# Transposing y one slot later and running the MLP's second product two pieces behind its first

## The chip, the core and the metric

The kernel runs on one core of one Trainium2 chip. The metric is device time in microseconds for one whole call, given as the median of several runs; the span from the first instruction to the last is a little shorter. The engines that matter here are TensorE (PE in the profile; its weight loads are a row of their own, PEld), VectorE (DVE), ScalarE (ACT) and GpSimd (POOL). SyncE (SP) issues most transfers.

## What is computed

Three layers follow one another on 3072 tokens of width 320 (batch 4, 768 steps, 8 heads of 40): a recurrence with a state per head, an MLP whose activation is the square of relu, and a mixture of 8 experts with one expert per token.

```python
# recurrence, per batch and head, for t in 0..767
y[t]   = r[t] @ state
Sa     = state @ a[t]
state  = state * w[t][None, :] - outer(Sa, b[t]) + outer(v[t], k[t])

# MLP, w_in 320x2048, w_out 2048x320
h = x @ w_in
g = np.maximum(h, 0.0) ** 2
x = g @ w_out

# mixture: 8 experts, capacity 768, w1 320x1024, w2 1024x320
expert = argmax(x @ w_gate); gate = softmax(x @ w_gate)[expert]
out = gate * (relu(x_e @ w1[expert]) @ w2[expert])
```

All values are float32. The products of MLP and experts are formed from high and low parts: a number is split into a rounded high part (written by ScalarE as fp32r) and the rest (subtracted on VectorE), and three of the four partial products are added.

## The kernel before

**Recurrence (class `Rwkv`).** The 768 steps are cut into 12 segments `s` of 64 steps, and a segment into two chunks `c` of 32 steps. In a chunk the steps are solved together, for which each segment needs the inverse of a triangular 32x32 matrix per head and batch. `invert` (from L194) forms it on GpSimd: 31 steps, each a product (`tmp`) and a subtraction (`solve_tl`), all recorded at L289 and all chained to one another. Ahead of it stands `lower` (from L173): PE makes `pa`, ACT copies a part of it (`solve_ab`, L185) and DVE masks and transposes it (`am`, L187; `a`, L191; `solve_al`, L198). Behind it, `inverted` (L214) transposes the result on DVE (`solve_tf`, L219) into `tt` (L222, L223), and `solve` applies it (`psa`). The state is carried on by `zv`, `zk`, `pz`, `pn` and `psd`. `products` (L116) prepares the decays of a coming segment by two scans on DVE: `rq_r` (L124, followed by a clamp L133 and a reciprocal L134) and `rq_q` (L137). `out` makes y of a chunk: `py` on PE, `y` on DVE (L388).

**MLP (class `Mlp`).** The 256 tokens of a segment (64 steps, 4 batches) go through 8 pieces `fp` of 256 hidden columns. `add_y` turns y by three transposes on PE (`pt`, L454) and splits it (ACT L459 to L461, DVE L462, L463). `up` makes a piece's first product in two halves of 8 matmuls (`pl`, L447), then relu on ACT (L645), relu times `pl` on DVE (`g`, L647), and its split: `gh` on ACT (L409), `gl` on DVE (L410). `down` makes the second product in two halves of 6 matmuls (`acc`, L629), with the high weights `woh` and a transferred low part `wol`. It runs one piece behind `up` (`self.last`). `gh` and `gl` have two buffers each, which the conversion of weights at the start also uses (`a`, `raw`, `mh`, `ml`, L517 to L551).

**Mixture (class `Moe`).** 15 units of 256 gathered tokens, with its own `up` and `down` (`upl`, `uacc`), which take over the same one-piece delay.

**What sets the order.** Only TensorE's instructions keep the program's order (`keep_in_program_order`), and GpSimd's are chained one behind another (`issue_after`). On DVE and ACT a scheduler chooses the order when the kernel is built. The main loop has slots `slot_a` to `slot_g` for each chunk; after each, `mlp(n)` puts in `n` halves of MLP pieces, by the table `SLOTS` (`SECOND` for segment 1, `FIRST` for 0). So TensorE alternates between recurrence and MLP. After the last segment the remaining pieces of the MLP run beside the routing of the tokens, then the mixture alone.

Of the kernel before, what the change touches and what calls it, by code (L numbers as in the profile page):

```python
# [30 lines left out]
C = 32  # L31
# [41 lines left out]
class Rwkv:  # L73
# [6 lines left out]
    def __init__(self, ctx, tc, ps, consts, keep, wd, kb, ad, rv, wl, tok, vt, rng):  # L80
        self.tc, self.nc, self.ps = tc, tc.nc, ps
        self.c = consts
        self.src = dict(wd=wd, kb=kb, ad=ad, rv=rv, wl=wl, tok=tok, vt=vt)
        nc = self.nc
        p1 = ctx.enter_context(tc.tile_pool(name="rw1", bufs=1))
        self.p = ctx.enter_context(tc.tile_pool(name="rwr", bufs=1))
# [127 lines left out]
    def inverted(self, s):  # L214
# [6 lines left out]
        tt = self.tile([128, C, NC, H], f"tt.{s}", 2)  # L221
# [159 lines left out]
    def out(self, s, c):  # L381
# [5 lines left out]
        y = self.tile([128, DM + 64], f"y.{s}_{c}", 2)  # L387
# [82 lines left out]
class Mlp:  # L470
# [28 lines left out]
    def tile(self, shape, name, tag, bufs, dt=F32):  # L499
        return self.p.tile(shape, dt, tag=tag, name=name, bufs=bufs)  # L500
# [101 lines left out]
    def load_gate(self):  # L602
        self.turn = self.routed = self.done = 0
        self.wo = {}
        self.last = self.slow = self.behind = None
# [30 lines left out]
    def up(self, s, x, fp, wol):  # L636
# [10 lines left out]
        nc.vector.tensor_tensor(out=g, in0=pl, in1=g, op=ALU.mult)  # L647
        gh = self.tile([128, 2, NT], f"gh{s}_{fp}", "gh", 2, F32R)
        gl = self.tile([128, 2, NT], f"gl{s}_{fp}", "gl", 2, F32R)
        self.behind = split(nc, gh, gl, g)  # L650
        self.last = partial(self.down, s, fp, gh, gl, wol)
        yield

    def down(self, s, fp, gh, gl, wol):
        if fp == 0:
            self.acc = [self.psa.tile([128, DX], F32, tag=f"acc{t}", name=f"acc{s}_{t}") for t in range(2)]
        for f in range(2):
            ft = fp * 2 + f
            for t in range(2):
                cols = slice(t * 128, (t + 1) * 128)  # L660
                for n, (a, b) in enumerate(((gh, self.woh[:, ft]), (gl, self.woh[:, ft]), (gh, wol[:, f]))):
                    self.mm(self.acc[t], lhsT=a[:, f, cols], rhs=b,
                            start=ft == 0 and n == 0, stop=ft == NFT - 1 and n == 2)
# [17 lines left out]
    def bursts(self, s, x):  # L681


        for fp in range(NFT // 2):
            last = self.last
            yield from self.routers(2 * fp + 2)
            yield from self.up(s, x, fp, self.low(s, fp))
            if last:
                yield from last()


class Slow:
# [53 lines left out]
    def mlp(self, ctx, y, w_in, w_out, w_gate, x1, logits):  # L746
# [13 lines left out]
        with tc.tile_pool(name="slm", bufs=2) as p, tc.For_i(0, NS, 1) as s:  # L760
# [10 lines left out]
            for fp in range(NFT // 2):  # L771
                for _ in ml.up("f", x, fp, ml.low("f", fp)):
                    pass
                for _ in ml.last():
# [3 lines left out]
        ml.last = ml.behind = None  # L778
# [3 lines left out]
class Moe:  # L782
# [426 lines left out]
    def unit(self, j, units):  # L1209
# [7 lines left out]
        for fp in range(FE // 256):  # L1217
# [3 lines left out]
            last, ml.last = ml.last, partial(self.down, j, w2, h, fp)  # L1221
            yield
            if last:
                yield from last()
# [7 lines left out]
    def run(self, units):  # L1232
        if not self.ml.last:
# [8 lines left out]
        for _ in self.ml.last():  # L1242
            pass
        self.ml.last = None
# [17 lines left out]
def const_arrays():  # L1262
# [5 lines left out]
        ident=np.eye(128),  # L1268
        mlow=s[None, :] < t[:, None],
        mup=t[:, None] < s[None, :],  # L1270
        lane=np.ones((128, 1)),
# [16 lines left out]
    for n, parts in enumerate((one, two)):  # L1288
# [8 lines left out]
AHEAD = 5000  # L1297
USUAL = 15
FIRST_UNITS, NE = 3, 10
# [36 lines left out]
def tile_rwkv__mlp__moe(ctx, tc, wd, kb, ad, rv, wl, tok, vt, nat, w_in, w_out, w_gate, w1, w2, cap, cst1, cst2, out):  # L1336
# [9 lines left out]
    with ExitStack() as ph:  # L1346
# [4 lines left out]
        rw = Rwkv(rp, tc, ps, consts, keep, wd, kb, ad, rv, wl, tok, vt, rng)  # L1351
# [48 lines left out]
        for s in range(NS):  # L1400
# [3 lines left out]
            for c in range(NC):  # L1404
                last, y = ys, None
                more = s + 1 < NS

                def others(half):
# [22 lines left out]
                def slot_c():  # L1431
                    if s > 1:
# [6 lines left out]
                def slot_d():  # L1439
                    rw.turn(s, c)  # L1440
# [129 lines left out]
_INS = ["wd", "kb", "ad", "rv", "wl", "tok", "vt", "nat", "w_in", "w_out", "w_gate", "w1", "w2", "cap", "cst1", "cst2"]  # L1570
# [3 lines left out]
def arrays(inputs):  # L1574
# [6 lines left out]
    d["cst1"], d["cst2"] = const_arrays()  # L1581
# [20 lines left out]
```

## Time and profile before

| what | value |
|---|---|
| median of 3 runs | 1127.3 us (1125.11 to 1129.19) |
| the profiled execution, its own time | 1132.63 us |
| its span (first to last instruction) | 1130.8 us |
| mean granted TensorE clock | 0.937 of full speed |
| busy: PE, PEld, DVE, ACT, POOL | 914.1, 854.5, 848.6, 570.4, 537.8 us |

The page gives busy time by engine and, for groups of instructions, the idle time of the engine ahead of them with what ended it. Idle time alone is no cost: it counts only where it lies on the chain of work that ends last. The table of the chain of waits follows that chain back from the last instruction. A timeline lists instructions in order of start, with the idle time of the engine before one in brackets and what released it. "x2" means that two instructions of one kind are listed as one row.

### The profile page before, as it was taken

The page shows a single profiled execution, that of the slowest core. Times are in us where ns is not written, and L with a number is a line of the kernel's source. Part 1 is how long each engine was busy: PE and PEld are TensorE (multiplying, and loading weights), DVE is VectorE, ACT ScalarE, POOL GpSimd, SP SyncE. Part 2 cuts the span into 40 slices and gives each one's busy share as a digit, 9 for nine tenths or more (in the row PEclk, how much of TensorE's full clock was granted, in tenths as well). Part 3 has the DMA queues.
Part 4 walks back from the last instruction along what each step waited for, and adds up shares of the span by engine and source line. Part 5 has one row for each costly group of instructions (what it writes and reads, how often), then busy time and mean ns, then how long its engine had stood idle before and what let it go on. Part 6 is the DMA issues. An engine that isn't in the chain of part 4 may idle for free.

```text
span 1130.8 us, 38768 instructions
## 1 busy us (share of the span) xinstructions
PE 914.1 (81%) x15962; PEld 854.5 (76%) x15962; DVE 848.6 (75%) x1807; ACT 570.4 (50%) x1570; POOL 537.8 (48%) x866
## 2 busy tenths in 40 slices
PE   1645535877988979797989798999999998999992
PEld 1545435767877969687978788899989998899992
DVE  7868966678787877778786878757777967777860
ACT  2435424444454454454545454555464667667750
POOL 4793851818385765739393939380010132223220
PEclk9999997988898989888988899999999999999997
DMA  8833634843353534443544345344194576677720
GB/s 225 217 95 103 154 96 119 275 126 114 107 158 102 163 100 136 126 115 108 152 120 135 119 123 152 98 121 119 56 327 120 161 220 191 195 209 236 226 80 9
DMA packets 85968, 164.19 MB, mean 145 GB/s; under 512 B 15565, under 2 KB 45903, under 8 KB 84816
## 3 DMA queue, kind: packets, MB, share of 16 engines
q1 hardware_dynamic: 76848, 141.52, 43.1%
q10 hardware_dynamic: 6048, 11.06, 3.6%
q0 software_dynamic: 2880, 8.98, 2.3%
q8 instruction: 129, 2.11, 0.8%
q14 instruction: 63, 0.52, 0.2%
HBM read 137.34 MB, written 16.24 MB: 136 GB/s over the span
## 4 chain that ended last, share of the span: by engine, by line
POOL 37%; PE 26%; DVE 12%; issue 9%; DMA 7%; ACT 3%; SPq 0%; POOLq 0%; DVEq 0%; ACTq 0%
POOL solve_tl L289 19%; POOL tmp L289 18%; PE upl L447 6%; PE uacc L1127 6%; PE pl L447 5%; PE acc L629 4%; DMA out_dram<-uo,room 4%; DMA xg<-x_dram,room 2%; DVE a L191 1%; PE pa L292 1%; DVE zv L348 1%; DVE solve_tf L219 1%; DVE g L647 1%; DVE gl L410 1%; DVE a L348 1%
## 5 line engine op out<-in xcount | busy, mean ns | idle before, releaser
L289 POOL TENSOR_TENSOR solve_tl<-solve_tl,tmp 128x126 f32<-128x126 f32 (+22 forms) x372 | 229.2, 616 | 29.1
L289 POOL TENSOR_TENSOR tmp<-solve_al,solve_tl 128x126 f32<-128x126 f32 (+22 forms) x372 | 210.2, 565 | 39.9 <-DVE a L191 11.7
L629 PE MATMUL acc<-woh,gh 128*128 128x328 f32 x384 | 134.5, 350 | 52.1 <-ACT gh L409 51.5
L629 PE MATMUL acc<-woh,gl 128*128 128x328 f32 x384 | 129.9, 338 | 12.7 <-DVE gl L410 12.1
L629 PE MATMUL acc<-wol,gh 128*128 128x328 f32 x384 | 126.5, 329 | 0.0
L447 PE MATMUL pl<-x_lo,wi_hi 128*128 128x256 f32 x384 | 113.3, 295 | 14.0 <-DVE x_lo L462 14.0
L447 PE MATMUL pl<-x_hi,wi_hi 128*128 128x256 f32 x384 | 120.4, 313 | 0.7 <-ACT x_hi L459 0.7
L629 PEld LDWEIGHTS acc<-woh,gh 128*128 128x128 f32 x384 | 77.5, 202 | 57.3 <-ACT gh L409 53.9
L447 PE MATMUL pl<-x_hi,wi_lo 128*128 128x256 f32 x384 | 112.9, 294 | 0.0
L1205 POOL DMA_INDIRECT out_dram<-uo,room x30 | 33.8, 1125 | 153.3 <-DVE uo L1194 82.7
L647 DVE TENSOR_TENSOR g<-pl,g 128x512 f32<-128x512 f32 x96 | 65.7, 684 | 49.2 <-ACT g L645 48.8
L645 ACT ACTIVATE g<-pl 128x512 f32<-128x512 f32 x96 | 57.2, 596 | 86.7 <-PE pl L447 85.0
L410 DVE TENSOR_TENSOR gl<-g,gh 128x512 fp32r<-128x512 f32 x96 | 66.6, 694 | 43.9 <-ACT gh L409 43.5
L289 POOL MEMSET solve_tl<- 128x512 f32 x12 | 6.8, 563 | 194.0 <-DVE solve_al L198 177.5
L409 ACT CAST gh<-g 128x512 fp32r<-128x512 f32 x96 | 59.3, 618 | 73.4 <-DVE g L647 69.7
L1135 POOL DMA_INDIRECT xg<-x_dram,room x30 | 30.5, 1017 | 135.1 <-DVE room L967 56.1
L629 PEld LDWEIGHTS acc<-woh,gl 128*128 128x128 f32 x384 | 78.0, 203 | 19.5 <-DVE gl L410 19.2
L447 PEld LDWEIGHTS pl<-x_lo,wi_hi 128*128 128x128 f32 x384 | 77.7, 202 | 14.3 <-DVE x_lo L462 14.3
L1127 PE MATMUL uacc<-w2h,hh 128*128 128x320 f32 x240 | 76.9, 320 | 10.5 <-DVE uo L1194 9.1
L447 PEld LDWEIGHTS pl<-x_hi,wi_hi 128*128 128x128 f32 x384 | 77.3, 201 | 4.5 <-ACT x_hi L459 1.1
L629 PEld LDWEIGHTS acc<-wol,gh 128*128 128x128 f32 x384 | 78.2, 204 | 0.0
L447 PEld LDWEIGHTS pl<-x_hi,wi_lo 128*128 128x128 f32 x384 | 77.6, 202 | 0.0
(263 smaller groups left out, 2783.9 us busy)
## 6 DMA issues: line engine op xcount, KB each, us to landing
wol<-wol SPq DMA_DIRECT2D x96, 328.0 KB
w<-in_w_dram SPq DMA_DIRECT2D x30, 640.0 KB
w<-in_w_dram SPq DMA_DIRECT2D x30, 512.0 KB
zv<-in_vt_dram SPq DMA_DIRECT2D x48, 208.0 KB
kb_d<-in_kb_dram SPq DMA_DIRECT2D x24, 320.0 KB
zk<-in_tok_dram SPq DMA_DIRECT2D x48, 160.0 KB
rx<-rt SPq DMA_DIRECT2D x192, 40.0 KB
w<-in_w_dram SPq DMA_DIRECT2D x30, 256.0 KB
```

The costliest lines, as they stand in the source:

```text
L191: nc.vector.transpose(out=ak[:, 0], in_=am[BY_STEP[j]])
L289: self.last = f(*a, **k).ins
L348: self.nc.vector.tensor_mul(v, v, w)
L409: return (nc.scalar.copy(hi, x).ins, nc.vector.tensor_tensor(out=lo, in0=x, in1=hi.bitcast(F32), op=ALU.subtract).ins)
L410: nc.vector.tensor_tensor(out=lo, in0=x, in1=hi.bitcast(F32), op=ALU.subtract).ins)
L447: tc.keep_in_program_order(tc.nc.tensor.matmul(out, lhsT=a, rhs=b, start=n == 0, stop=n == len(seq) - 1))
L629: self.tc.keep_in_program_order(self.nc.tensor.matmul(*a, **k))
L645: nc.scalar.activation(g, pl, AF.Relu)
L647: nc.vector.tensor_tensor(out=g, in0=pl, in1=g, op=ALU.mult)
L1127: self.tc.keep_in_program_order(self.nc.tensor.matmul(*a, **k))
L1135: nc.gpsimd.indirect_dma_start(out=xg[:, 0:DX], out_offset=None, in_=self.x1, in_offset=bass.IndirectOffsetOnAxis(ap=self.idx[2 * j + t], ...
L1205: self.nc.gpsimd.indirect_dma_start(out=self.out, out_offset=bass.IndirectOffsetOnAxis(ap=self.to[:, n:n + 1], axis=0), in_=o[:, t], in_of ...
```

## The change

1. `add_y` of a chunk moves from `slot_b`, ahead of `solve`, to `slot_c` for chunk 0 (ahead of `lower`) and to `slot_d` for chunk 1. In segment 1, chunk 0 it stays. `y` and `tt` go from two buffers to one.
2. `down` runs two pieces behind `up` (`BEHIND = 2`, a list `pending`); in the mixture the delay stays at one piece (`drain(1)`), so that after the mixture's first `up` two pieces of `down` stand in a row. Within `down`, the order is now `gh` by high and low weights for both halves of the tokens, then `gl`. The transfer of `wol` is issued one burst later, still one piece ahead of its use.
3. ACT squares relu straight into `gh`. DVE's product for `g` comes behind that (it overwrites relu), then `gl`. ACT and DVE keep their counts of operations.
4. `gh` and `gl` get three buffers. Some constants move into an array of their own (`cst3`, 128x70), loaded on ACT's queue.

```diff
+        ct = p1.tile([128, cst.shape[1]], F32, name="ct3")
+        nc.scalar.dma_start(out=ct, in_=cst)
...
-        tt = self.tile([128, C, NC, H], f"tt.{s}", 2)
+        tt = self.tile([128, C, NC, H], f"tt.{s}", 1)
...
-        y = self.tile([128, DM + 64], f"y.{s}_{c}", 2)
+        y = self.tile([128, DM + 64], f"y.{s}_{c}", 1)
...
     def tile(self, shape, name, tag, bufs, dt=F32):
+        bufs = BUFS.get(tag, bufs)
...
-        nc.vector.tensor_tensor(out=g, in0=pl, in1=g, op=ALU.mult)
         gh = self.tile([128, 2, NT], f"gh{s}_{fp}", "gh", 2, F32R)
         gl = self.tile([128, 2, NT], f"gl{s}_{fp}", "gl", 2, F32R)
-        self.behind = split(nc, gh, gl, g)
-        self.last = partial(self.down, s, fp, gh, gl, wol)
+        square = nc.scalar.activation(gh, g, AF.Square).ins
+        nc.vector.tensor_tensor(out=g, in0=pl, in1=g, op=ALU.mult)
+        self.behind = (square, nc.vector.tensor_tensor(out=gl, in0=g, in1=gh.bitcast(F32), op=ALU.subtract).ins)
+        self.pending.append([self.down, s, fp, gh, gl, None])
...
-            for t in range(2):
-                cols = slice(t * 128, (t + 1) * 128)
-                for n, (a, b) in enumerate(((gh, self.woh[:, ft]), (gl, self.woh[:, ft]), (gh, wol[:, f]))):
...
+            parts = (0, gh, self.woh[:, ft]), (1, gh, wol[:, f]), (2, gl, self.woh[:, ft])
+            for n, a, b, t in [(*p, t) for ps in (parts[:2], parts[2:]) for t in range(2) for p in ps]:
...
-            last = self.last
             yield from self.routers(2 * fp + 2)
-            yield from self.up(s, x, fp, self.low(s, fp))
-            if last:
-                yield from last()
+            self.lows()
+            yield from self.up(s, x, fp)
+            yield from self.drain(BEHIND)
+
+    def drain(self, n):
+
+        while len(self.pending) > n:
+            self.lows()
+            f, *a = self.pending.pop(0)
+            yield from f(*a)
...
+BUFS = dict(gh=3, gl=3)
+BEHIND = 2
...
                 def slot_b():
-                    if y is not None:
-                        ml.add_y(xs[last[0]], last[1], y)
+                    nonlocal y
                     if s == 1 and c == 0:
+                        add()
+                        y = None
...
                 def slot_c():
+                    add()
                     if s > 1:
...
                 def slot_d():
+                    if c == 1:
+                        add()
                     rw.turn(s, c)
```

TensorE around the solution of segment 7, before: `acc5` is the second product of the MLP for segment 5, `pt` turns y, `psa7` applies the inverse, `pz` belongs to the state.

```order
L629 MATMUL acc5_0_7615<-wol5_5_7981,gh5_5_8075 128x328
L629 MATMUL acc5_1_7616<-woh_88,gh5_5_8075 128x328
L629 MATMUL acc5_1_7616<-woh_88,gl5_5_8076 128x328
L629 MATMUL acc5_1_7616<-wol5_5_7981,gh5_5_8075 128x328
L454 MATMUL pt_8252<-ct_60,y_6_1_8202 128x128 x3
L292 MATMUL psa7_0_8261<-rh_7_0_8238,tt_7_8125 32x40 x32
L270 MATMUL pz6_1_0_0_8301<-ct_60,zv0_114 104x40
L270 MATMUL pz6_1_0_1_8302<-ct_60,zv0_114 104x40
```

The same place after: half a piece of the first product (`pl5_7`) stands ahead of `psa7`, whose line is now L294.

```order
L449 MATMUL pl5_7_8242<-x_hi_5990,wi_lo_492 128x256
L449 MATMUL pl5_7_8242<-x_mx_5992,wi_mx_493 128x256
L449 MATMUL pl5_7_8242<-tops0_99,wi_mx_493 128x256
L294 MATMUL psa7_0_8251<-rh_7_0_8234,tt_7_8121 32x40 x32
L272 MATMUL pz6_1_0_0_8291<-ct_60,zv0_116 104x40
L272 MATMUL pz6_1_0_1_8292<-ct_60,zv0_116 104x40
```

The turning of y follows some rows later, behind 8 matmuls of `pl5_7` and 12 of `acc5`, and directly ahead of `pa8`, which starts the next inverse:

```order
L633 MATMUL acc5_1_7682<-wol5_5_8067,gh5_5_7990 128x328
L633 MATMUL acc5_0_7681<-woh_88,gl5_5_7991 128x328
L633 MATMUL acc5_1_7682<-woh_88,gl5_5_7991 128x328
L456 MATMUL pt_8334<-ct_60,y_6_1_8198 128x128 x3
L294 MATMUL pa8_0_8344<-kb_d_113,a0_114 32x64 x32
L294 MATMUL pa8_1_8385<-kb_d_113,a0_114 32x64 x32
```

Between `pz` and `pa8` there were 16 matmuls of `pl` and 6 of `acc` before; now it is 8, 12 and the three transposes.

VectorE from the end of inverse 7 on, before (order's rows call a scan SCALAR_TENSOR_TENSOR; `rq10_q8` and `rq16_r9` are the scans, and stand ahead of these rows):

```order
L219 STREAM_TRANSPOSE solve_tf7_8123<-solve_tl7_7346 128x1024
L647 TENSOR_TENSOR g5_6_8153<-pl5_6_8136,g5_6_8153 128x512
L388 TENSOR_TENSOR y_6_1_8202<-py6_1_8169,qt_6_1_7077 128x320
L223 SCALAR_TENSOR_TENSOR tt_7_8125<-solve_tf7_8123,ct_60,tt_7_8125 128x512
L243 STREAM_TRANSPOSE qt_8_0_9246<-rq10_q8_8797 128x8x32
L244 STREAM_TRANSPOSE qt_8_0_9246<-rq10_q8_8797 128x8x8
L410 TENSOR_TENSOR gl5_6_8157<-g5_6_8153,gh5_6_8156 128x512
L348 TENSOR_TENSOR zv0_114<-zv0_114,g64_7_6883 40x8x2x40 x2
L282 TENSOR_TENSOR zk1_120<-zk1_120,rx_7_1_8690 64x2x8x40 x2
```

The same engine and place after:

```order
L221 STREAM_TRANSPOSE solve_tf7_8119<-solve_tl7_7342 128x1024
L245 STREAM_TRANSPOSE rt_8_1_8793<-rq10_r8_8586 128x8x32
L246 STREAM_TRANSPOSE rt_8_1_8793<-rq10_r8_8586 128x8x8
L139 SCALAR_TENSOR_TENSOR rq10_q8_8796<-wl_8_8065,seed_q_111 128x650
L225 SCALAR_TENSOR_TENSOR tt_7_8121<-solve_tf7_8119,ct3_106,tt_7_8121 128x512
L123 MEMSET seed_q_111 104x16
L660 TENSOR_TENSOR g5_6_8141<-pl5_6_8124,g5_6_8141 128x512
L390 TENSOR_TENSOR y_6_1_8198<-py6_1_8165,qt_6_1_7073 128x320
L126 SCALAR_TENSOR_TENSOR rq16_r9_8803<-w_d_112,seed_q_111 104x1040
L661 TENSOR_TENSOR gl5_6_8144<-g5_6_8141,gh5_6_8143 128x512
L350 TENSOR_TENSOR zv0_116<-zv0_116,g64_7_6879 40x8x2x40 x2
L284 TENSOR_TENSOR zk1_122<-zk1_122,rx_7_1_8676 64x2x8x40
```

The scans, with two transposes, a memset, a clamp and a reciprocal that belong to them, have moved from ahead of `solve_tf` to behind it. It is so for the inverses 3 to 9; after inverse 10 only `rq10_q` has moved.

## Rows read from the trace of the kernel before

**Rows 1.** Page, chain that ended last: share of the span by engine.

```profile
POOL 37%; PE 26%; DVE 12%; issue 9%; DMA 7%; ACT 3%; SPq 0%; POOLq 0%; DVEq 0%; ACTq 0%
```

**Rows 2.** Waits of PE, 200 to 720 us: total us, times, longest.

```profile
PE acc L629 <- ACT gh L409: 35.9, 9, 4.8
PE pt L454 <- DVE y L388: 12.5, 7, 4.9
```

**Rows 3.** Timeline of POOL: first product of inverses 3 and 8.

```profile
252.78 0.24 POOL L289 TENSOR_TENSOR tmp<-solve_al,solve_tl 128x31 f32<-128x31 f32 x1 [1.68 <-DVE a L191]
555.45 0.24 POOL L289 TENSOR_TENSOR tmp<-solve_al,solve_tl 128x31 f32<-128x31 f32 x1 [0.35 <-DVE a L191]
```

**Rows 4.** Windows: us; busy PE, PEld, DVE, ACT, POOL; PEclk; DMA; GB/s.

```profile
555.45:597.71 42.26, 35.94 (x834) 32.81 (x833) 33.26 (x51) 18.89 (x46) 37.47 (x62) 0.92 0.52 149
676.25:715.60 39.35, 35.65 (x833) 32.76 (x832) 29.50 (x48) 18.01 (x45) 34.56 (x62) 0.96 0.50 144
477.57:496.79 19.22, 16.30 (x331) 14.71 (x330) 14.44 (x25) 11.55 (x31) 0.87 (x4) 0.82 0.38 103
538.86:555.45 16.59, 15.65 (x464) 14.64 (x454) 14.23 (x25) 11.45 (x31) 1.05 (x4) 1.00 0.40 111
527.58:533.25 5.67, 5.67 (x122) 5.38 (x114) 5.45 (x8) 1.73 (x6) 5.36 (x5) 0.71 0.50 149
830.00:834.00 4.00, 3.74 (x17) 3.47 (x17) 3.31 (x13) 3.14 (x11) 0.00 (x0) 0.65 1.05 393
```

**Rows 5.** Timeline of DVE between inverses 7 and 8.

```profile
539.08 1.25 DVE L219 STREAM_TRANSPOSE solve_tf<-solve_tl 128x1024 f32<-128x1024 f32 x1 [1.09 <-POOL solve_tl L289]
...
547.99 0.69 DVE L647 TENSOR_TENSOR g<-pl,g 128x512 f32<-128x512 f32 x1 [0.97 <-ACT g L645]
549.37 0.69 DVE L410 TENSOR_TENSOR gl<-g,gh 128x512 fp32r<-128x512 f32 x1 [0.68 <-ACT gh L409]
```

**Rows 6.** Timeline of DVE inside inverse 7: the two scans.

```profile
528.18 1.61 DVE L137 TENSOR_TENSOR_SCAN rq_q<-wl,seed_q 128x650 f32<-128x650 f32 x1
...
529.98 2.33 DVE L124 TENSOR_TENSOR_SCAN rq_r<-w_d,seed_q 104x1040 f32<-104x1040 f32 x1
```

**Rows 7.** Timeline of POOL at the same time.

```profile
527.57 0.40 POOL L289 TENSOR_TENSOR solve_tl<-solve_tl,tmp 128x110 f32<-128x110 f32 x1
...
528.50 1.50 POOL L289 TENSOR_TENSOR solve_tl<-solve_tl,tmp 128x108 f32<-128x108 f32 x1
530.08 2.37 POOL L289 TENSOR_TENSOR tmp<-solve_al,solve_tl 128x96 f32<-128x96 f32 x1
532.53 0.77 POOL L289 TENSOR_TENSOR solve_tl<-solve_tl,tmp 128x96 f32<-128x96 f32 x1
```

**Rows 8.** Timeline of DVE between inverses 1 and 2, while POOL is idle.

```profile
161.90 0.41 DVE L520 SCALAR_TENSOR_TENSOR a<-raw,a 128x256 uint32<-128x256 uint32 x1
...
165.89 1.50 DVE L137 TENSOR_TENSOR_SCAN rq_q<-wl,seed_q 128x650 f32<-128x650 f32 x1
...
169.24 2.32 DVE L124 TENSOR_TENSOR_SCAN rq_r<-w_d,seed_q 104x1040 f32<-104x1040 f32 x1
```

**Rows 9.** Timeline of PE between inverses 6 and 7.

```profile
481.44 0.73 PE L454 MATMUL pt<-ct,y 128*128 128x128 f32 x3 [2.21 <-DVE y L388]
...
484.82 0.58 PE L447 MATMUL pl<-x_hi,wi_hi 128*128 128x256 f32 x1
...
488.40 0.47 PE L629 MATMUL acc<-woh,gh 128*128 128x328 f32 x1
...
490.08 1.99 PE L292 MATMUL pa<-kb_d,a 40*32 40x64 f32 x128
```

**Rows 10.** Waits of PE, 817 to 862 us.

```profile
PE acc L629 <- ACT gh L409: 2.8, 2, 1.7
PE acc L629 <- DVE gl L410: 0.9, 3, 0.3
```

**Rows 11.** Timeline of PE between inverses 1 and 2.

```profile
181.08 0.64 PE L629 MATMUL acc<-woh,gh 128*128 128x328 f32 x1 [12.76 <-ACT gh L409]
```

More of the change, by code (lines that the diff above doesn't have):

```diff
@@ L604, in load_gate @@
         self.wo = {}
-        self.last = self.slow = self.behind = None
+        self.slow = self.behind = None
+        self.pending = []
         for k in range(3):
@@ L634, in low, with lows, up @@
         return wol
-    def up(self, s, x, fp, wol):
+    def lows(self):
+        for p in self.pending:
+            if p[-1] is None:
+                p[-1] = self.low(*p[1:3])
+    def up(self, s, x, fp):
         nc, NT = self.nc, self.NT
@@ L658, in down @@
             ft = fp * 2 + f
-            for t in range(2):
-                cols = slice(t * 128, (t + 1) * 128)
-                for n, (a, b) in enumerate(((gh, self.woh[:, ft]), (gl, self.woh[:, ft]), (gh, wol[:, f]))):
-                    self.mm(self.acc[t], lhsT=a[:, f, cols], rhs=b,
-                            start=ft == 0 and n == 0, stop=ft == NFT - 1 and n == 2)
+            parts = (0, gh, self.woh[:, ft]), (1, gh, wol[:, f]), (2, gl, self.woh[:, ft])
+            for n, a, b, t in [(*p, t) for ps in (parts[:2], parts[2:]) for t in range(2) for p in ps]:
+                self.mm(self.acc[t], lhsT=a[:, f, t * 128:(t + 1) * 128], rhs=b,
+                        start=ft == 0 and n == 0, stop=ft == NFT - 1 and n == 2)
             if f == 0:
@@ L771, in mlp @@
             for fp in range(NFT // 2):
-                for _ in ml.up("f", x, fp, ml.low("f", fp)):
+                for _ in ml.up("f", x, fp):
                     pass
-                for _ in ml.last():
+                for _ in ml.drain(0):
                     pass
@@ L777, in mlp @@
         nc.sync.dma_start(out=logits, in_=lgd)
-        ml.last = ml.behind = None
+        ml.behind = None
         return ps, ml
@@ L1220, in unit @@
             h = self.up(j, x, w, fp)
-            last, ml.last = ml.last, partial(self.down, j, w2, h, fp)
+            ml.lows()
+            ml.pending.append([self.down, j, w2, h, fp])
             yield
-            if last:
-                yield from last()
+            yield from ml.drain(1)
             for _ in range(5):
@@ L1232, in run @@
     def run(self, units):
-        if not self.ml.last:
+        if not self.ml.pending:
             self.ml.behind = None
@@ L1241, in run @@
             yield from self.unit(j, units)
-        for _ in self.ml.last():
+        for _ in self.ml.drain(0):
             pass
-        self.ml.last = None
     def others(self):
@@ L1268, in const_arrays @@
         ident=np.eye(128),
+        lane=np.ones((128, 1)),
+    )
+    own = dict(
         mlow=s[None, :] < t[:, None],
         mup=t[:, None] < s[None, :],
-        lane=np.ones((128, 1)),
         par=np.stack([p // 16 % 2 == 0, p // 16 % 2 == 1], axis=1),
@@ L1287, in const_arrays @@
     out = []
-    for n, parts in enumerate((one, two)):
+    for n, parts in enumerate((one, two, own)):
         at = 0
@@ L1350, in tile_rwkv__mlp__moe @@
         rp = ph.enter_context(ExitStack())
-        rw = Rwkv(rp, tc, ps, consts, keep, wd, kb, ad, rv, wl, tok, vt, rng)
+        rw = Rwkv(rp, tc, ps, consts, keep, wd, kb, ad, rv, wl, tok, vt, rng, cst3)
         xs = {}
@@ L1406, in tile_rwkv__mlp__moe, with add @@
                 more = s + 1 < NS
+                def add():
+                    if y is not None:
+                        ml.add_y(xs[last[0]], last[1], y)
                 def others(half):
```

10 lines of the change are left out of this document (5 added, 5 removed).

## The prediction

> **What bounds the kernel now.** I began with the chain that ended last. GpSimd holds 37% of the span and TensorE 26% [rows 1], and the GpSimd part is the 31-step inverse. So the kernel has two stages: until the last inverse ends, the loop through GpSimd sets the pace; behind it, TensorE does.
>
> The loop next. The first product of inverse 3 starts at 252.78 us, that of inverse 8 at 555.45 [rows 3]. Five segments take 302.7 us, 60.5 each. A whole inverse lasts 42.3 us (the first line of [rows 4]), so 18.2 us are left between the end of one and the start of the next. I call that stretch the gap: the result is turned, `psa` and the state follow, then `pa`, its transposes, and GpSimd starts again. One gap took 16.6 us at full TensorE clock, another 19.2 us at a mean granted clock of 0.82 [rows 4].
>
> Then TensorE's waits in these segments: 35.9 us in 9 waits for `gh`, 12.5 us for y [rows 2]. They look like the prize, but the longest wait for `gh`, 4.8 us, and its kind lie while GpSimd works on an inverse, so that its end doesn't lead to the next start. What counts is what lies in the gap, and what lengthens the inverse.
>
> **Steady segments, the gap.** In the gap between inverses 7 and 8 DVE works 14.2 of 16.6 us [rows 4]: DVE is the engine that sets it at full clock. Its two waits in the middle, 0.97 and 0.68 us, are for relu and `gh` of the piece being made [rows 5]. With half a piece ahead of `psa`, `pl` ends 8 matmuls sooner, and relu and square lie beside DVE's work on `zk`; I take both waits away: -1.65. The order of the changed kernel puts both scans, with their clamp, reciprocal, transposes and memset, into the gap. Before, that run of instructions took 5.67 us (from 527.58 on, [rows 4]). It stood beside GpSimd there; with GpSimd idle the two scans take 1.50 and 2.32 us [rows 8] against 1.61 and 2.33 [rows 6], so I take 5.5. The gap becomes 16.6 - 1.65 + 5.5 = 20.4 us at full clock. The scans' inputs are ready long before, so none waits; but `tt` waits for the first scan, and all that hangs on `tt` and `zv` (`psa`, `pz`) starts 2 and 4 us later.
>
> That idles TensorE. Its work ahead of `psa` is 6 `acc` and 8 `pl`, about 2 us, while DVE needs 1.2 (`solve_tf`), 0.6 (transposes), 1.5 (scan) and 0.7 (`tt`); between `psa` and `pz` it waits again, for the second scan. In the gap of rows 9 an idle time of 2.21 us went before, and the 16 `pl` took from 484.82 to 488.40, 0.22 us each, the 6 `acc` 0.28 us each [rows 9], with a granted clock of 0.82 over the gap: the lower of the two levels, 1.2 GHz, while they ran. If that happens after the change, `pz` ends about 10.1 us into the gap (DVE's list summed up to `zv`), and then come 8 x 0.22 + 12 x 0.28 + 0.73 (`pt`) = 5.9 us to `pa`, at 16.0; from `pa` to GpSimd's start the same gap needed 6.7 us (490.08 to 496.79): 22.6 us. So the gap goes from 16.6 to 20.4 at full clock, from 19.2 to 22.6 at the lower one: +3.4 to +3.8, and +4.4 against the mean if all gaps run at the lower level.
>
> **Steady segments, the inverse.** GpSimd's steps are stretched while DVE scans: 1.50 us at 528.50 and 2.37 at 530.08, where its neighbour took 0.40, then 0.77 beside the clamp [rows 6, 7]. The excess is 1.1 + 2.0 + 0.4 = 3.5 us, and it leaves the inverse with the scans. The trace has a direct witness: the inverse that starts at 676.25 has no `rq_r` scan beside it and takes 39.35 us instead of 42.26 [rows 4], 2.9 less where my sum for that scan and its clamp says 2.4. So between 3.5 and 4.0 us are won per inverse; I take 3.9, since the witness is a whole window. DVE's waits for `gh` inside the inverse go too, but what DVE does earlier there stretches GpSimd all the same: nothing.
>
> The Trainium skill, "SBUF — State Buffer", section "Who interferes with whom", says that a DVE instruction with two SBUF inputs and a GpSimd instruction that reads SBUF exclude each other, and its summary advises to schedule whichever is off the critical path. Rows 6 and 7 agree on the exclusion. By the advice this move would be wrong in the gap, where DVE is on the path: it pays 5.5 us of DVE to save 3.9 us of GpSimd, and only the 1.65 us of waits make it even.
>
> Per segment this is +3.4 to +4.4 in the gap and -3.5 to -4.0 in the inverse. I take +3.9 and -3.9: 0, over seven segments between -4 and +6. After inverse 10 only `rq_q` moves: +2.1 (scan and transposes) - 1.1 = +1.
>
> **The start.** Between inverses 1 and 2 TensorE stood 12.76 us until the first `gh` [rows 11], with `pa` of the next inverse queued behind that product. With `down` two pieces behind, a third `up` stands there instead, which needs only the first `g`; up to 5 us of this gap can go (`gh` came that much behind the rest of DVE's queue). Against it, DVE does eight or nine more weight conversions of 0.41 us [rows 8] ahead of inverse 1: +3.5; and one more scan pair stays in the third gap: up to +2. The new small transfer for constants hides behind the larger first loads. Sum 0, with 5 us to either side.
>
> **Behind the recurrence.** From there TensorE is the bound and its waits count. Between 817 and 862 us it waited 2.8 us for `gh` and 0.9 for `gl` [rows 10]: ACT was held by the gather of tokens, and the second product stood right behind. With two pieces between they are covered: -3.7. At 830 to 834 us the granted clock was 0.65 [rows 4], behind those waits; that is 4 x 0.35 = 1.4 us of full-speed work, which goes with its cause. The other edits here are neutral: as many matmuls, and squaring on ACT for a cast of the same size. Term: -5.1, between 0 (a new wait) and -6. In the mixture the delay is as before: 0.
>
> **Sum.** 0 + 1 + 0 - 5.1 = -4.1 us against the profiled 1132.6, so 1128.5 there; taken from the median of 1127.3, **1123.2 us**.
>
> **Rivals.**
>
> *A, the gap stays at full clock.* If TensorE's idle times don't bring the lower level, all gaps take 20.4 us: 20.4 + 38.4 = 58.8 per segment, -1.7 x 7 = -12, with the rest -16: 1111 us. For it speaks that the waits of 4.8 us inside the inverse, and the low stretches that follow them, go. Against it: idle times of 2 to 4 us will stand in each gap.
>
> *B, the gap is slower than the inverse gains.* All gaps run at the lower level, with `pa` behind 12 `acc` and `pt`: 22.6 + 38.8 (a saving of 3.5) = 61.4, +0.9 x 7 = +6; the start costs its 3 to 5, and the last stage gives 3: +7, **1134 us**. It decides from a gap of 22 us on. For it: the low stretches in the gap of rows 9, after less idle time than the change makes. The Trainium skill, "TensorE: Matmul & The Clock Gate", section "What's actually happening", holds the throttled state to be the default that activity releases; the trace agrees as far as the clock of 0.82 in that gap goes.
>
> *C, a wash.* The steady segments gain nothing, the start costs some 3 us, the last stage gives 3 to 5: 1124 to 1130. Nothing in the profile speaks against it; the two large terms cancel within their own error.
>
> *D, the waits were the bound.* If TensorE's 48 us for `gh` and y in the recurrence [rows 2] were on the path, most would go: 1085 to 1100. The chain names GpSimd, not these waits, and there is no room in the loop for them: gap and inverse fill the 60.5 us.
>
> **How the numbers follow.** A measurement of this kernel can tell about 0.3% (3.4 us) from no change. Forecast, 1117 to 1124: 0.28; A, 1106 to 1117: 0.13; C: 0.30; B, 1130 to 1140: 0.25; D: 0.04. Faster by over 0.3%: 0.45; same 0.30; slower 0.25. The range takes the forecast, C, and the nearer halves of A and B: 1111 to 1135; the likeliest case alone has 1117 to 1124.
>
> **What would show it.** Right: inverses of some 38.5 us and gaps of 20.4 to 22.6, with a period near 60.5; both scans between two inverses; no wait for `gh` over 1 us in the recurrence; 817 to 862 without waits for `gh` and `gl`. The first step is wrong if inverses stay near 42 (then something else of DVE stretches GpSimd) or if gaps stay near 18 (the scans run where TensorE was the bound). A new wait at `psa` for `tt`, or at `pa`, is where rival B would show; a shorter time with unchanged period would mean that start and end were mis-sized.

## The result

The change made the kernel slower: 1136.6 us in the median (1133.9 to 1142.3, 20 runs) against 1127.0 (1121.0 to 1137.3, 20 runs), a ratio of 1.0088 with a 95% interval of 1.0069 to 1.0108. I had forecast 1123.2. The time lies beyond the range, on the other side, near the 1134 of rival B, and in good part for a reason that rival B did not name. The profiled execution has a span of 1138.5 us and a mean granted clock of 0.923.

The page of the changed kernel first: the chain, then the group that answers to the longest waits of before (busy, mean ns, then idle time of the engine ahead of it with what ended it).

```profile
PE 29%; POOL 29%; DVE 15%; issue 11%; DMA 8%; ACT 4%; POOLq 0%; DVEq 0%; SPq 0%; ACTq 0%
...
L633 PE MATMUL acc<-woh,gh 128*128 128x328 f32 x384 | 133.1, 352 | 2.8 <-ACT x L686 2.8
```

The wait for `gh` of [rows 2] is gone altogether: `acc` waits 2.8 us in the whole span, and for something else. GpSimd's share of the chain fell from 37% [rows 1] to 29%. Each inverse became some 4 us shorter, but that is less than half of the difference; the rest is that the chain, as the profile follows it, passes two inverses fewer through GpSimd. So the share itself proves little.

TensorE didn't come to wait less in the recurrence. Its longest waits from 200 to 720 us in the changed kernel are new ones (total us, times, longest):

```profile
PE pz L272 <- DVE zv L350: 29.3, 16, 3.5
PE psa L294 <- DVE seed_q L123: 17.9, 7, 4.0
...
PE psa L294 <- DVE tt L225: 10.6, 2, 7.8
```

In the kernel before, the waits of `psa` there were this one:

```profile
PE psa L292 <- DVE tt L223: 1.0, 1, 1.0
```

All of TensorE's waits in that stretch add up to 84 us now and 75 us before. So the change took away the waits that it was meant to take away, put others in their place, and the kernel became slower.

Which stage? Windows of the changed kernel, an inverse and the gap ahead of it (us; busy time of PE, PEld, DVE, ACT, POOL; granted clock; DMA share; GB/s):

```profile
551.11:589.54 38.43, 35.56 (x836) 33.22 (x836) 27.79 (x44) 19.45 (x49) 33.64 (x62) 0.96 0.51 144
528.67:551.11 22.44, 16.90 (x386) 15.83 (x374) 19.24 (x32) 10.27 (x27) 0.87 (x4) 0.85 0.36 96
```

The inverse takes 38.4 us instead of 42.3, the gap 22.4 instead of 16.6 to 19.2 [rows 4]. DVE works 19.2 us in the gap instead of 14.2. From inverse 3 (248.86 us) to inverse 10 (673.46) a segment takes 60.66 us. The last inverse ends at 762.99; before, at 764.17. So at the end of the recurrence the changed kernel was level or 1 us ahead, and at the end of the span it was 7.7 us behind. In this pair of executions the loss shows behind the recurrence, where I had forecast a gain of 5.1.

TensorE's waits from 764 to 870 us of the changed kernel, and windows there:

```profile
PE ea_inv L1143 <- DVE solve_op L965: 3.4, 1, 3.4
PE acc L633 <- ACT x L686: 2.8, 1, 2.8
```

```profile
764.00:820.00 56.00, 52.28 (x1147) 49.13 (x1141) 35.30 (x97) 28.12 (x70) 0.00 (x0) 1.00 0.25 75
820.00:830.00 10.00, 8.39 (x39) 6.18 (x40) 5.77 (x26) 0.97 (x3) 2.14 (x2) 0.51 0.36 122
830.00:870.00 40.00, 36.89 (x274) 36.38 (x273) 29.27 (x82) 27.36 (x77) 1.96 (x2) 1.00 0.89 280
```

The waits for `gh` and `gl` of [rows 10] are gone here too. In their place stands a wait of 3.4 us for `solve_op`, and behind it ten microseconds at a granted clock of 0.51. `solve_op` belongs to the early routing: when segment 9 has left the MLP, the tokens of the first ten segments are ranked (`ea_rank`), and matrices that DVE makes (`solve_op`, `rq_op`) are multiplied on TensorE (`ea_inv`) to find which tokens the first units gather. DVE and TensorE there, in the changed kernel:

```profile
820.85 3.21 DVE L965 TENSOR_SCALAR solve_op<-ct,room 128x128 fp32r<-128x128 f32 x16
...
821.27 3.12 PE L1143 MATMUL ea_inv<-solve_op,rq_ov 128*6 128x128 f32 x16 [3.37 <-DVE solve_op L965]
```

and in the kernel before, where DVE began 7 us ahead of TensorE:

```profile
810.43 3.22 DVE L949 TENSOR_SCALAR solve_op<-ct,room 128x128 fp32r<-128x128 f32 x16
...
817.39 0.89 PE L1127 MATMUL ea_inv<-solve_op,rq_ov 128*6 128x128 f32 x12
```

The routing starts on a condition, `ml.done == NE`, that is, when the second product of segment 9's last piece has run. With the second product two pieces behind, that is a piece later, two slots. `ea_inv`, though, keeps its fixed place in TensorE's order, behind the recurrence: in the trace of before 447 matmuls lie between the last `ea_rank` and the first `ea_inv`, in that of the changed kernel 267. This was my first theory, called late routing below: the routing starts later, its consumer doesn't. Two rivals: the two pieces of second product that are left over at the end, and a mixture that runs worse for itself.

### The profile page after: what moved, and what is told of

Read it like the earlier page. It is cut to its first block, busy times and chain, and to the rows that moved or that the text cites. A ratio compares the mean times of both kernels' runs of the same rounds, so it can differ in the third digit from the quotient of the medians.

```text
span 1138.5 us, 38822 instructions
## 1 busy us (share of the span) xinstructions
PE 910.7 (80%) x15962; PEld 858.3 (75%) x15962; DVE 850.1 (75%) x1807; ACT 572.0 (50%) x1570; POOL 503.7 (44%) x866
## 4 chain that ended last, share of the span: by engine, by line
PE 29%; POOL 29%; DVE 15%; issue 11%; DMA 8%; ACT 4%; POOLq 0%; DVEq 0%; SPq 0%; ACTq 0%
POOL solve_tl L291 15%; POOL tmp L291 14%; PE acc L633 7%; PE pl L449 6%; PE upl L449 5%; PE uacc L1143 5%; DMA out_dram<-uo,room 3%; DMA xg<-x_dram,room 2%; DVE rq_r L126 2%; DVE zv L350 1%; DVE rq_q L139 1%; DMA zk<-in_tok_dram 1%; DVE a L193 1%; PE pt L456 1%; PE pn L294 1%
## 5 line engine op out<-in xcount | busy, mean ns | idle before, releaser
L291 POOL TENSOR_TENSOR solve_tl<-solve_tl,tmp 128x126 f32<-128x126 f32 (+22 forms) x372 | 211.0, 567 | 29.2
L291 POOL TENSOR_TENSOR tmp<-solve_al,solve_tl 128x126 f32<-128x126 f32 (+22 forms) x372 | 195.5, 526 | 40.7 <-DVE a L193 12.5
L633 PE MATMUL acc<-woh,gl 128*128 128x328 f32 x384 | 95.5, 332 | 0.0
L1143 PE MATMUL uacc<-w2h,hl 128*128 128x320 f32 x240 | 75.5, 315 | 0.0
L1143 PE MATMUL uacc<-w2l,hh 128*128 128x320 f32 x240 | 75.2, 313 | 0.0
L633 PEld LDWEIGHTS acc<-woh,gl 128*128 128x128 f32 x384 | 71.6, 207 | 0.0
```

Source lines behind the costliest of these rows:

```text
L291: self.last = f(*a, **k).ins
L633: self.tc.keep_in_program_order(self.nc.tensor.matmul(*a, **k))
L1143: self.tc.keep_in_program_order(self.nc.tensor.matmul(*a, **k))
```

## The experiments

Stages of every profiled execution, all in us. "To 3" is the start of the first product of inverse 3; "3 to last" goes from there to the end of the last inverse; "segment" is a seventh of the time from inverse 3 to inverse 10; "to MLP end" goes from the last inverse's end to the last `acc`; "rest" from there to the end of the span. Median and ratio are those of the timed runs, the ratio against the kernel before on the same chip, with its interval.

| kernel | to 3 | 3 to last | segment | to MLP end | rest | span | median | ratio |
|---|---|---|---|---|---|---|---|---|
| before | 252.8 | 511.4 | 60.50 | 99.2 | 267.5 | 1130.8 | 1127.0 | |
| before again (f2) | 252.1 | 508.6 | 60.16 | 104.3 | 262.4 | 1127.4 | 1129.2 | |
| changed | 248.9 | 514.1 | 60.66 | 105.6 | 269.9 | 1138.5 | 1136.6 | 1.0088 (1.0069 to 1.0108) |
| changed again (f3) | 250.2 | 515.0 | 60.78 | 105.9 | 265.2 | 1136.3 | 1139.0 | 1.0110 (1.0075 to 1.0145) |
| e1 routing early | 248.6 | 513.6 | 60.59 | 96.1 | 268.5 | 1126.8 | 1129.1 | 0.9997 (0.9975 to 1.0019) |
| e2 before, routing late | 252.5 | 504.0 | 59.47 | 109.1 | 262.7 | 1128.3 | 1132.6 | 1.0042 (1.0018 to 1.0066) |
| e3 one piece behind | 246.3 | 509.4 | 60.08 | 96.2 | 266.5 | 1118.4 | 1123.0 | 0.9965 (0.9927 to 1.0002) |
| e4 y early | 249.0 | 503.4 | 59.20 | 103.4 | 267.9 | 1123.7 | 1126.6 | 0.9985 (0.9956 to 1.0014) |
| f1 y and routing early | 247.5 | 503.9 | 59.30 | 96.4 | 263.7 | 1111.5 | 1116.4 | 0.9894 (0.9845 to 0.9943) |
| h1 scans inside | 247.6 | 512.6 | 60.60 | 105.6 | 267.1 | 1132.9 | 1136.0 | 1.0064 (1.0038 to 1.0089) |
| h2 f1, scans inside | 244.0 | 504.3 | 59.42 | 96.4 | 270.6 | 1115.2 | 1114.7 | 0.9885 (0.9843 to 0.9927) |
| i1 y behind pa | 247.1 | 518.4 | 61.12 | 100.3 | 266.6 | 1132.4 | 1137.5 | 1.0108 (1.0069 to 1.0148) |
| g2 squaring alone | 247.9 | 507.3 | 59.82 | 93.6 | 270.0 | 1118.8 | 1120.5 | 0.9941 (0.9917 to 0.9966) |
| j1 only chunk 1's y late | 245.8 | 505.6 | 59.77 | 96.5 | 264.2 | 1112.1 | 1114.0 | 0.9861 (0.9816 to 0.9907) |

### Routing early, in the changed kernel (e1)

```diff
-            yield from self.drain(BEHIND)
+            yield from self.drain(0 if s == NE - 1 and fp == NFT // 2 - 1 else BEHIND)
```

> The changed kernel, but after the last piece of segment 9 all waiting second products run at once, so that segment 9 ends, and the routing of its tokens begins, in the slot in which it does in the kernel before. Late routing (my theory: the time was lost because the routing starts two slots later while TensorE meets its products at the old place): the 3.4 us wait of TensorE for solve_op and the stretch at the lower clock behind it (820 to 830 us) go, the MLP ends some 8 us sooner, and the time is 8 to 10 us below the changed kernel, 1126 to 1130, level with before. Rival 1 (the two pieces of second product that lie behind at the end cost the time): the MLP ends as late as in the changed kernel, 1134 to 1138. Rival 2 (the mixture itself runs worse): the same 1134 to 1138, with the difference behind 870 us.

Measured: 1129.1 us, ratio 0.9997 to the kernel before. Windows of it where the changed kernel had lost its clock, and DVE's row:

```profile
764.00:820.00 56.00, 55.27 (x1110) 52.41 (x1097) 40.49 (x119) 27.87 (x71) 1.33 (x2) 1.00 0.30 86
820.00:830.00 10.00, 8.27 (x63) 8.04 (x62) 6.60 (x17) 7.39 (x22) 0.81 (x1) 1.00 1.04 327
```

```profile
807.40 3.23 DVE L965 TENSOR_SCALAR solve_op<-ct,room 128x128 fp32r<-128x128 f32 x16
```

`solve_op` comes at 807.4 instead of 820.9, the clock stays at 1.00, and the MLP ends 96.1 us behind the last inverse instead of 105.6. Every other stage is within 1.5 us of the changed kernel. In the changed kernel, late routing costs 9.5 us; both rivals expected no change, and fall.

### Routing late, in the kernel before (e2)

```diff
                     if not more and side is None and ml.done == NE:
-                        side = mo.early(rw)
+                        held += 1
+                        if held > 2:
+                            side = mo.early(rw)
```

> The kernel before, with one thing added: the early routing starts two slots after segment 9 has ended instead of at once. Late routing: TensorE waits 3 us or more for solve_op, the clock falls behind it, and the time rises by 6 to 10 us to 1133 to 1137. Rivals 1 and 2: the routing has slack and the time stays within 2 us of 1127.

Measured: ratio 1.0042, about 4.7 us slower. The suspected cost, put alone into the kernel before, shows the same two rows: a wait for `solve_op`, here of 3.4 us, and the clock behind it (0.66 over the ten microseconds from 813):

```profile
PE ea_inv L1127 <- DVE solve_op L949: 3.4, 1, 3.4
```

```profile
813.00:823.00 10.00, 9.37 (x51) 7.14 (x52) 5.07 (x24) 1.28 (x4) 2.14 (x2) 0.66 0.47 145
```

It is less than the 6 to 10 us expected, and the end of the MLP varies between executions of the kernel before itself (99.2 and 104.3). The later of the two (f2) has a wait of `acc` for `gh` of 4.1 us, where the first profile has 1.2, and behind it a granted clock of 0.66 from 851 to 861 us. e2 has such a wait too, of 3.3 us, so f2 is the fairer partner: e2's MLP ends 4.8 us later than f2's, as much as the timed runs say. So late routing costs some 5 us in the kernel before and 9.5 in the changed one.

### One piece behind, in the changed kernel (e3)

```diff
-BEHIND = 2
+BEHIND = 1
```

> The changed kernel with the second product one piece behind the first, as before; y is still turned one slot later, ScalarE still squares. In the order VectorE's scans stand inside the inverse again and the routing starts in its old slot. Late routing: the loss goes, time within 4 us of before (1123 to 1131), inverses near 42 us and gaps near 18 us. If instead the later turning of y or the squaring were the loss, the time stays at 1133 to 1138.

Measured: ratio 0.9965 (0.9927 to 1.0002), inverses of 41.6 us, gaps of 17 to 19, MLP end at 96.2. As expected, and it tells a second thing: it was the distance of two pieces that moved the scans into the gap, for here the turning of y and the squaring are as in the change, and the scans are back inside.

### y early, in the changed kernel (e4)

```diff
                 def slot_b():
-                    nonlocal y
+                    add()
                     if s == 1 and c == 0:
-                        add()
-                        y = None
...
                 def slot_c():
-                    add()
...
                 def slot_d():
-                    if c == 1:
-                        add()
```

> The changed kernel with y turned in its old slot, ahead of the solution (one buffer of y and tt as in the change); second product two pieces behind, squaring kept. Late routing: the routing starts as late as in the change, so the time stays at 1133 to 1139, and the period of the recurrence at 60 to 61 us, since the scans stay in the gap. If the later turning of y is the loss: 1125 to 1130.

Here my theory missed. The routing is late in this kernel too, the end of the MLP is at 103.4, and yet the time is some 10 us below the changed kernel, level with before. The gain lies in the recurrence: 59.20 us per segment against 60.66, 503.4 us from inverse 3 to the last against 514.1. Windows of it, same inverse and gap as shown above for the changed kernel:

```profile
545.09:582.70 37.61, 34.27 (x809) 31.79 (x810) 28.90 (x44) 19.88 (x49) 32.83 (x62) 1.00 0.53 146
524.02:545.09 21.07, 17.30 (x460) 15.82 (x459) 19.15 (x32) 10.23 (x27) 0.89 (x5) 0.84 0.39 103
```

DVE works as long in the gap, 19.15 against 19.24 us, but the gap is 1.4 us shorter. So there are two costs of about 10 us each, and a gain that had hidden one of them. A place where they could be seen is the end of the gap. DVE in the changed kernel, where y is turned directly ahead of `pa`:

```profile
545.10 0.42 DVE L464 TENSOR_TENSOR x_lo<-pt,x_hi 128x256 fp32r<-128x256 f32 x1 [1.61 <-ACT x_mx L463]
545.44 0.27 DVE L465 TENSOR_TENSOR x_mx<-pt,tops 64x128 fp32r<-64x128 f32 x1
545.75 1.40 DVE L350 TENSOR_TENSOR a<-a,g 40x512 f32<-40x512 f32 x2
```

and in e4, where `x_lo` had been made long before:

```profile
539.72 1.41 DVE L350 TENSOR_TENSOR a<-a,g 40x512 f32<-40x512 f32 x2 [0.87 <-PE pa L294]
```

TensorE at the same place, in the changed kernel:

```profile
543.75 0.49 PE L456 MATMUL pt<-ct,y 128*128 128x128 f32 x3
544.16 1.99 PE L294 MATMUL pa<-kb_d,a 40*32 40x64 f32 x128
```

and in e4:

```profile
538.57 1.99 PE L294 MATMUL pa<-kb_d,a 40*32 40x64 f32 x128
```

In the changed kernel DVE waits 1.61 us for ACT's copies of the turned y, and the decay of `a`, the masks and the transposes that GpSimd waits for are queued behind it. The decay starts 17.1 us into the gap; in e4, 15.7. Most of the 1.61 us is no cost, though, for the decay waits for `pa` in any case, as the row of e4 shows. `pa` starts 15.5 us into the gap here and 14.6 in e4, and the decay follows 1.6 and 1.2 us behind that. So of the 1.4 us, 0.9 lie on TensorE ahead of `pa`: `pt` takes 0.4, and the 8 `pl` and 12 `acc` behind `pz` take 5.1 us instead of 4.6, with more of them at the lower clock. Only 0.4 are DVE's `x_lo` and `x_mx`. Over the seven gaps from inverse 3 to 10 the two parts are 0.6 and 0.4 us in the mean; the remaining 0.4 us per segment are inverses of 38.3 us against 37.9.

e3 and g2 (below) differ in the same way, y late or early, with the second product one piece behind: 60.08 against 59.82 us per segment. So the late turning cost 1.4 us together with the distance of two pieces and little without it; there is one profiled execution of each kernel for this, and why it is so stays open.

### Both early (f1), and the kernel before again (f2)

The two edits above in one kernel.

> The two edits of the first runs together: the changed kernel with y turned in its old slot and the second products of segment 9 run out at its end. If late routing (some 9 us behind the recurrence) and the late turning of y (some 1.4 us per segment in the gap) are separate costs, they add: period near 59.2 us, end of the MLP some 96 us behind the last inverse, 1115 to 1120 us, faster than both kernels. If they were one and the same (either edit only moves the end of segment 9 against the recurrence), the time is that of either edit alone, 1125 to 1130.

Measured: ratio 0.9894 (0.9845 to 0.9943), 1116.4 us. The costs add: 503.9 us from inverse 3 to the last as in e4, MLP end at 96.4 as in e1.

The kernel before was run once more for its profile.

> The kernel before once more, for the profile. Its recurrence took 60.5 us per segment in the first profile; the kernel with late routing, whose recurrence is the same program, took 59.5. If the kernel before runs at 59.5 here, the recurrence of the changed kernel (60.6 twice) costs 1 us per segment against it; at 60.5 it costs nothing.

60.16 us per segment. With the 60.50 of the first profile and the 59.47 of e2, which is the same program up to there, the kernel before takes 504 to 511 us from inverse 3 to the last. The changed kernel takes 514 to 515, and e1 and h1 513 to 514. So the recurrence of the changed kernel is slower than before, by 3 to 11 us; from the first profile alone, 2.7, that could not be told. From inverse 3 on, the gaps add up to 178 us in both executions of the changed kernel, against 144, 142 and 138 before, and the inverses to 336 or 337, against 366 or 367: the gaps lose more than the inverses win.

### The scans back inside the inverse (h1, h2)

```diff
-            self.rt[s, c] = self.by_step(r, 1 + c * C, f"rt.{s}_{c}", 2)
+            self.rt[s, c] = self.by_step(r, 1 + c * C, f"rt.{s}_{c}", 3)
```

> The changed kernel with a third buffer for the turned decays (rt), by which the order puts VectorE's two scans back inside the inverse; all else as in the change. My sum: inverses go from 38 to about 42 us, gaps from 22.4 to about 18.5, period within 1 us of 60.6, time within 6 us of the changed kernel. If the scans in the gap are the loss: period 59 or less and 1123 to 1128. If they are a gain: period 62 or more and over 1145.

> The first kernel of this call with the third rt buffer, so the scans inside the inverse, with y turned early and routing early. Same sum: inverses near 42, gaps near 17.5, within 5 us of that kernel.

h2 is the kernel f1 with this edit. With a third buffer for the turned decays the order puts both scans ahead of `solve_tf` again, with all else as in the change. Windows of h1, the same inverse and gap:

```profile
551.31:592.68 41.37, 36.91 (x845) 34.34 (x843) 32.19 (x49) 20.19 (x50) 36.59 (x62) 0.96 0.55 155
531.95:551.31 19.36, 15.17 (x324) 14.30 (x325) 14.92 (x27) 9.75 (x26) 0.87 (x4) 0.74 0.29 81
```

3 us longer inside, 3 us shorter outside: 60.60 us per segment against 60.66, and in h2 59.42 against 59.30. Where the scans stand makes no difference to the loop that these runs can tell. That step of the prediction holds.

### y behind pa (i1)

The kernel of e1, with the y that is turned in chunk 0 turned behind `lower` and `invert` in the late slot instead of ahead of them:

```diff
                 def slot_c():
-                    add()
+                    x = xs[last[0]] if y is not None else None
...
                         rw.invert(s + 1)
+                    if x is not None:
+                        ml.add_y(x, last[1], y)
```

> As the kernel with routing early (e1), but within the late slot of chunk 0, y is turned behind the matrices of the next inverse (pa) instead of ahead of them, so that the turning, ACT's copies and VectorE's x_lo no longer stand ahead of the decay of a. If the 1.4 us per segment of the late turning are VectorE's wait for ACT's copy of the turned y (1.6 us in the changed kernel) with a, am and the transposes queued behind it: period 59.4 or less, 8 to 10 us below e1, 1117 to 1121. If the late slot costs for another reason (y read later, TensorE idle ahead of psa at the lower clock): period 60.3 to 60.7, 1126 to 1131.

A miss: 1137.5 us and 61.12 per segment. The wait of the decay for `x_lo` is gone, but the gap is longer:

```profile
528.03:551.49 23.46, 17.48 (x444) 15.89 (x439) 20.91 (x36) 10.15 (x27) 0.88 (x5) 0.92 0.48 128
```

DVE now has 36 instructions and 20.9 us of work in the gap, against 32 and 19.2: the scheduler moved others in. And TensorE waits for `x_lo` itself, in the next piece's first product, where there was no such wait in this stretch before (waits of PE from 200 to 720 us):

```profile
PE pl L449 <- DVE x_lo L464: 22.5, 8, 6.0
```

So this kernel moved the wait rather than took it away, and added work of its own: `psa` starts 6.5 us into the gap in the mean, against 4.1 in e1. The decay does follow `pa` by 1.2 us again, as in e4, instead of 1.6: that is the 0.4 us that `x_lo` and `x_mx` had cost, far less than the 1.61 us of DVE's wait that I had expected to win.

### Only chunk 1's y late (j1)

The kernel of e1, with the y that is turned in chunk 0 (the one in the gap) in its old slot, and that of chunk 1 a slot later as in the change:

```diff
                 def slot_b():
                     nonlocal y
-                    if s == 1 and c == 0:
+                    if c == 0:
                         add()
                         y = None
+                    if s == 1 and c == 0:
...
                 def slot_c():
-                    add()
```

> As the kernel with routing early (e1), but only the y that is turned in chunk 1 stays a slot later; the one turned in chunk 0, which in the change stands at the end of the gap ahead of pa, is back ahead of psa. If the gap is where the late turning costs: gaps of 21 us, period 59.2 to 59.5, 1115 to 1121, as with both back (f1). If chunk 1's late turning costs it, inside the inverse's time: gaps of 22.4 us, period 60.3 to 60.7, 1126 to 1131, as e1.

Measured: 1114.0 us, ratio 0.9861 (0.9816 to 0.9907), 505.6 us from inverse 3 to the last against 513.6 in e1. The segment of 59.77 is a little above what I expected and the time a little below, near that of both back (f1). So what costs is the turning in chunk 0, at the end of the gap; the other costs nothing that these runs can tell. It has the lowest ratio of the study, some 15 us below the kernel before, though the intervals of f1 and h2 overlap with its own.

### Changed again (f3), and squaring alone (g2)

> The changed kernel once more, beside the others on one chip: 1134 to 1140, period 60.6, end of the MLP 104 to 106 us behind the last inverse; a check on how far its stages vary between executions.

The changed kernel again took 60.78 us per segment, 105.9 to the MLP's end, and 1139.0 us.

In g2 y is turned early (as in e4) and the second product is one piece behind (as in e3); of the change there remain the squaring on ACT, the order within the second product, the buffers and the constants.

> The changed kernel with the second product one piece behind and y in its old slot: of the change there are left ScalarE's squaring, the order of the second product's matmuls, the third buffers of gh and gl, the single buffers of y and tt, and the constants. If the distance of two pieces brings the gain behind the recurrence: MLP end as in before (99 to 104 us behind the last inverse) and 1122 to 1128. If squaring and buffers bring it: about 96 us and 1114 to 1120.

Measured: ratio 0.9941 (0.9917 to 0.9966), 1120.5 us, MLP end at 93.6, the earliest of all. So the gain behind the recurrence, which I had put down to the distance of two pieces, comes without it. Which of the things that remain brings it, the squaring, the order or the buffers, no run tells. With the distance (e4) the MLP ends 9.8 us later, the segment is 0.6 us shorter, and the time some 5 us longer by the ratios. With the distance and the routing in time (f1) the MLP ends 2.8 us later than in g2 and the segment is 0.5 us shorter; the intervals of the two ratios overlap.

## Why the prediction was wrong, step by step

**The inverse.** Right. From 42.3 to 38.4 us; I took 3.9 off.

**The gap.** Right as a size, 21.6 to 22.9 us in the changed kernel, 22.4 in the mean, against 20.4 to 22.6. That is the upper end, my sum for the lower clock, and its working held: `pz` ends 10.1 us into the gap, as summed. My list of what moves had a hole: I carried the three matmuls of `pt` to the new place, with 0.73 us on TensorE, and not what follows them, ACT's three copies and DVE's `x_lo`, which stands ahead of the decay of `a`. That part is worth 0.4 us per segment. The late turning as a whole costs 0.8 to 1.5 us per segment (e4, f1, j1), 8 to 11 us from inverse 3 to the last; most of that was in my sum, but I never set it against a kernel that leaves y where it was.

**Per segment.** I took 0 and had -4 to +6 for seven segments. Against the first profile it was +1 (60.66 against 60.50), against the three executions of that program +4 in the mean (424.6 us against 423.5, 421.1 and 416.3). The range held it, but the 0 in the sum was too low: the gaps lost 4.3 to 5.2 us each, where I took 3.9, and the inverses won 3.9 to 4.2. That the two sides of the scans cancel is shown by h1 and h2.

**The start.** I took 0 with 5 to either side. Inverse 3 starts 2 to 4 us sooner (248.9 and 250.2 against 252.1 to 252.8): a gain.

**Behind the recurrence.** This is the step that failed. I wrote -5.1 us, between 0 and -6; measured, the MLP ends 105.6 and 105.9 us behind the last inverse against 99.2 and 104.3 before, a loss of 1 to 7 us. In the mean of two executions of each kernel, the start gives -2.9 us, the recurrence +4.6, this stage +4.0 and the rest +2.6, where I had 0, +1, -5.1 and 0: this is the largest miss. The waits did go, and the gain is real: with the routing in time the MLP ends 96 us behind the last inverse (e1, f1, h2, j1, e3). It isn't the gain of two pieces, though, since g2 has it with one; I had called the other edits neutral. And I had looked at what waits in this stage, not at what starts it. The delay of the second product is also a delay of `done`, and `done` starts the routing, two slots later, against a consumer with a fixed place. DVE's lead over `ea_inv`, 7.0 us from start to start in the trace of before, is the slack that I should have read and set against two slots. `solve_op` came 10.4 us later (820.85 against 810.43): the lead was used up, with a wait of 3.4 us, and the clock fell behind it. e1 puts the whole at 9.5 us: from a gain to a loss. My bound of 0, "a new wait", had no size for that wait.

**The rivals.** B had the size and half of the place. It put +6 into the steady segments, with gaps of 22.6 us at the lower clock: the gaps came out at 22.4, the wait at `psa` that I had named as B's sign is there (28.5 us in 9 waits against 1.0 in one), and the recurrence takes 3 to 11 us more. But B had a loss at the start, which was a gain, and a gain of 3 in the last stage, where late routing stood; no rival named a wait at `ea_inv`. So it is partly luck that B's 1134 lies near. D: the 48 us of waits for `gh` and y left TensorE, and the time didn't fall. As others came in their place (84 us in all against 75), this alone doesn't settle D. A fell: the clock in the gaps went down, to 0.76 to 0.85.

**The mixture.** I took 0. "Rest" varies from 262 to 271 us among all kernels, and from 262 to 267 for the program of before alone. Whether the change costs a microsecond or two there stays open.

## What to carry to other kernels

When work is delayed by some slots, look for what its end sets off: a counter, a flag, a side task that starts on it; then read how much lead that task had over its consumer, and set it against the delay. When a step moves, follow its whole chain of instructions onto every engine's queue, to the last one that stands ahead of something on the path; and before a wait on one queue is called a cost, see whether the instruction behind it would have had to wait for another engine anyway. When waits leave an engine, add up all its waits again: others may have come. And try the parts apart: here two of them cost some 10 us each, while the kernels without both (f1, h2, j1) were 12 to 16 us faster than before.

## What the runs showed of the hardware

A wait of TensorE cost more than its length. Two things followed the 3.4 us at `ea_inv`. Its 16 products came no faster than DVE made `solve_op`, 3.12 us beside DVE's 3.21; before, with all of `solve_op` ready, 12 of them took 0.89. With four more for `rq_op`, `ea_inv` took 3.9 us instead of 1.5. And the granted clock was 0.51 for the ten microseconds from 820, that is at the lower of its two levels, 1.2 GHz. Two starts of `pl` lie 0.12 us apart ahead of the wait, and 0.21 behind it:

```profile
815.42 0.28 PE L449 MATMUL pl<-x_hi,wi_hi 128*128 128x256 f32 x1
815.54 0.28 PE L449 MATMUL pl<-x_lo,wi_hi 128*128 128x256 f32 x1
...
829.23 0.41 PE L449 MATMUL pl<-x_hi,wi_hi 128*128 128x256 f32 x1
829.44 0.41 PE L449 MATMUL pl<-x_lo,wi_hi 128*128 128x256 f32 x1
```

From such starts I estimate that the 6 `acc` and 13 `pl` from 825.7 to 830.3 took 2.1 us longer than at the full clock. Wait, slow products and clock make 3.4 + 2.4 + 2.1 = 7.9 of the 9.5 us by which the MLP ends sooner in e1; the rest isn't accounted for. I had priced such a stretch in the gaps, not behind a new wait.

The recurrence of one and the same program took 504 to 511 us in three executions. The gaps hold 6 of the 7 us (144.3 us in sum against 138.3 in e2), and their clock shows why: the gap between inverses 6 and 7, 19.2 us at a granted clock of 0.82 in the first profile of before [rows 4], took 17.4 us at 1.00 in e2, with the same instructions from `pt` to `pa` (the row counts 98 matmuls more, most of them `py` and `pr`, which ran just ahead of the window in the first profile):

```profile
473.97:491.40 17.43, 15.76 (x429) 14.27 (x417) 14.44 (x25) 11.47 (x31) 0.88 (x4) 1.00 0.36 98
```

So a stage of one profile can be 7 us off another of the same kernel, not much less than the whole effect of 9.6; the verdicts above rest on the timed runs, and on stages that came out alike in several kernels.
